# New constants in the table that orders the instructions of all engines: a two-layer attention and GEGLU kernel on one core

## The chip, the cores and the metric

The kernel runs on one core of a Trainium2 chip. A core has five engines with instruction queues of their own: TensorE (PE, with its weight loads shown apart as PEld), VectorE (DVE), ScalarE (ACT), GpSimd (POOL) and SyncE (SP), which only issues DMAs here. Matmuls write into PSUM, eight banks of 128 partitions x 512 fp32; DVE, ACT and POOL work on SBUF, and DVE and ACT read PSUM too. The metric is device microseconds of one execution; three executions of the kernel before gave 2450.06, 2450.28 and 2450.37.

## The reference

A residual block of attention and a residual block of a gated feed-forward network, each behind a layer norm without learned factors, are applied twice with the same weights. There are 2048 rows of 512 numbers, 32 heads of 16, and 1792 hidden columns.

```python
def _A_ref(x, wqkv, wo):                      # H = 32, Dh = 16
    qkv = (x @ wqkv).reshape(B, S, 3, H, Dh).transpose(2, 0, 3, 1, 4)
    q, k, v = qkv[0], qkv[1], qkv[2]
    scores = jnp.einsum("bhqd,bhkd->bhqk", q, k) * (Dh ** -0.5)
    p = _softmax(scores, axis=-1)
    o = jnp.einsum("bhqk,bhkd->bhqd", p, v)
    return o.transpose(0, 2, 1, 3).reshape(B, S, D) @ wo

def _B_ref(x, w_gate, w_up, w_down):
    return (_gelu(x @ w_gate) * (x @ w_up)) @ w_down

x = x + _A_ref(_layernorm(x, axis=-1), A_wqkv, A_wo)
x = x + _B_ref(_layernorm(x, axis=-1), B_w_gate, B_w_up, B_w_down)
x = x + _A_ref(_layernorm(x, axis=-1), A_wqkv, A_wo)
x = x + _B_ref(_layernorm(x, axis=-1), B_w_gate, B_w_up, B_w_down)
```

## The kernel before

The work of attention is cut into units: one block of query rows (512, at the end of the second layer 256, 128 and 128) by four heads, which stand in four groups of 32 partitions. Each unit goes through two passes.

The first pass finds the largest score of each row. PE multiplies 128 query rows with 512 keys for a head (L1910, one PSUM bank), and DVE takes the maximum (L1925), of one bank at a time or of two. To relieve DVE, some of these pieces are folded: POOL forms the difference of two blocks of keys (KD, L1522), PE multiplies it (L1725), ACT keeps its positive part (L1735), and one instruction of DVE (L1920, with a read of its accumulator) then gets the maximum of both blocks from one bank.

The second pass computes the scores again, transposed and with the maximum subtracted (L1782; a bank holds a tile, which is 1, 2 or 4 matmuls of 512, 256 or 128 columns). ACT takes the exponential of one bank or of two (L1758), and PE multiplies it with V and a column of ones (L1806) into the last bank. ACT copies the finished sums out (L1300), POOL divides (L1310, L1315).

Between these, as short chains of matmuls (L769), run the projections to K, Q and V, the output projection, and the feed-forward: the gate matmuls (WG) with GELU on ACT, the up matmuls (WU) with a product (on DVE L1473, or by ACT and POOL L1479 and L1481), the down matmuls (WD) and the addition to x (L1499 in the last layer, which also stores). For most rows GELU is made of tanh (L1394), which stands in the same table of ACT as the exponential. For the last 512 rows of the second layer the GELU table is loaded (L1460): once for 384 rows, in a run of 14 activations during which no exponential is issued, and once for the last 128 rows at the very end. Where PE would idle, it gets fill matmuls on zero weights (L1949), which compute nothing.

All this is put in order before the kernel runs, by a planner in Python. It keeps a clock for each engine with estimated durations, and at each step picks what PE does next: a piece of the first pass, of the second, both, a matmul of a chain, a product with V, or a fill. The instructions of the other engines follow from that. Each engine then runs its list from front to back and waits on semaphores. What the planner picks depends on 33 constants: how many banks each pass may hold (C1, C2 and their like), how long it waits for a second free bank before it takes one (S1D, DB1, S2D, DB2), how far one pass may run ahead of the other (LAG, LAGT, FL, GL), how soon chains are urgent (DUE, DUEM), how many matmuls of a chain go at once (PIECE, GP), and others. A row of the table PLAN holds a set of them. The first pass has 2048 pairs of score blocks; after every 16 of them, a stretch, the planner takes the next row:

```python
if pos["p1"] >= STRETCH * stretch[0]:
    if stretch[0] < len(PLAN):
        SPC, SPLIT, S1C, S2C, OV, LIM, NT, ..., CM, J1, J2 = PLAN[stretch[0]]
    stretch[0] += 1
```

A fill is issued only when PE's load over the last 3.4 us of the planner's clock is below a bound, which isn't in the table.

Of the kernel before, what the change touches and what calls it, by code (L numbers as in the profile page):

```python
# [22 lines left out]
    (0.15, 0.1, 0.55, 0.22, 0.0, -0.05, 2, 0, 30, 84, 13, 80, 0.2, 2.0, -5, 10, 1, 3, 7, 3, 0.1, 4, 3, 3, 3, 4, 0.42, 0.0, 0.42, 0.0, 2, 9.0, 9.0),  # L23
    (0.15, 0.1, 0.55, 0.32, 0.1, 0.0, 3, 0, 30, 50, 13, 80, 0.2, 2.0, 20, 10, 2, 1, 7, 2, 0.0, 4, 3, 3, 4, 4, 0.42, 0.0, 0.42, 0.0, 2, 9.0, 9.0),
    (0.15, 0.1, 0.55, 0.22, 0.0, -0.05, 2, 0, 30, 84, 13, 80, 0.2, 2.0, -5, 10, 2, 3, 7, 3, 0.1, 4, 3, 3, 3, 4, 0.6, 0.0, 0.42, 0.0, 2, 9.0, 9.0),
    (0.15, 0.1, 0.55, 0.22, 0.0, -0.05, 2, 0, 30, 84, 13, 80, 0.2, 2.0, -5, 10, 2, 3, 7, 3, 0.1, 4, 3, 3, 3, 4, 0.6, 0.0, 0.42, 0.0, 2, 9.0, 9.0),
    (0.15, 0.05, 0.55, 0.02, 0.0, -0.05, 3, 0, 30, 76, 13, 80, 0.3, 2.5, -5, 10, 2, 4, 7, 1, 0.1, 4, 3, 3, 3, 4, 0.6, 0.0, 0.42, 0.0, 2, 9.0, 9.0),
    (0.15, 0.05, 0.55, 0.02, 0.0, -0.05, 3, 0, 30, 76, 13, 80, 0.3, 2.5, -5, 10, 2, 4, 7, 1, 0.1, 4, 3, 3, 3, 4, 0.6, 0.0, 0.42, 0.0, 2, 9.0, 9.0),
    (0.15, 0.05, 0.55, 0.32, 0.0, -0.05, 2, 0, 30, 76, 13, 80, 0.2, 3.0, -5, 10, 2, 3, 3, 3, 0.1, 4, 3, 3, 3, 4, 0.8, 0.15, 0.42, 0.0, 2, 9.0, 1.1),
    (0.15, 0.05, 0.55, 0.02, 0.0, -0.1, 3, 0, 30, 76, 13, 80, 0.3, 2.5, -5, 10, 2, 3, 7, 3, 0.1, 4, 3, 2, 3, 4, 0.6, 0.0, 0.42, 0.15, 2, 9.0, 1.1),  # L30
    (0.15, 0.05, 0.55, 0.02, 0.0, -0.05, 3, 0, 30, 76, 13, 80, 0.3, 2.5, -5, 10, 2, 4, 7, 3, 0.1, 4, 3, 3, 3, 4, 0.6, 0.0, 0.42, 0.0, 2, 9.0, 9.0),
    (0.15, 0.05, 0.55, 0.32, 0.0, -0.05, 3, 0, 30, 76, 13, 80, 0.3, 2.5, 10, 10, 2, 3, 7, 3, 0.1, 4, 3, 3, 3, 4, 0.6, 0.0, 0.42, 0.0, 2, 9.0, 9.0),
    (0.15, 0.05, 0.55, 0.32, 0.0, -0.05, 2, 0, 30, 76, 13, 50, 0.2, 3.0, -5, 10, 2, 3, 9, 3, 0.1, 4, 3, 3, 3, 4, 0.8, 0.15, 0.42, 0.0, 2, 1.1, 9.0),
# [3 lines left out]
    (0.15, 0.05, 0.55, 0.32, 0.0, -0.1, 3, 0, 30, 76, 13, 80, 0.3, 2.5, 10, 10, 2, 3, 7, 3, 0.1, 4, 3, 3, 3, 4, 0.6, 0.0, 0.42, 0.0, 2, 9.0, 9.0),  # L37
    (0.15, 0.05, 0.55, 0.32, 0.0, -0.1, 3, 0, 30, 76, 13, 80, 0.3, 2.5, 10, 10, 2, 3, 7, 3, 0.1, 4, 3, 3, 3, 4, 0.6, 0.0, 0.42, 0.0, 2, 9.0, 9.0),
    (0.15, 0.05, 0.55, 0.32, 0.0, -0.05, 2, 0, 30, 76, 13, 80, 0.2, 3.0, -5, 10, 2, 3, 3, 3, 0.1, 4, 3, 3, 3, 4, 0.8, 0.15, 0.42, 0.0, 2, 1.1, 1.1),
    (0.15, 0.05, 0.55, 0.42, 0.2, -0.05, 2, 0, 30, 76, 13, 80, 0.2, 2.0, -5, 6, 2, 3, 3, 3, 0.0, 4, 3, 3, 3, 4, 0.42, 0.0, 0.42, 0.0, 2, 9.0, 9.0),  # L40
    (0.15, 0.05, 0.55, 0.42, 0.1, -0.05, 2, 0, 30, 76, 13, 80, 0.3, 2.0, -5, 6, 2, 2, 5, 3, 0.0, 4, 3, 3, 3, 4, 0.42, 0.0, 0.42, 0.0, 2, 9.0, 9.0),
    (0.15, 0.0, 0.55, 0.42, 0.1, -0.05, 3, 0, 30, 76, 13, 40, 0.7, 2.0, 10, 2, 2, 3, 5, 4, 0.0, 4, 3, 3, 3, 4, 0.42, 0.0, 0.42, 0.0, 2, 9.0, 9.0),
    (0.15, 0.0, 0.55, 0.42, 0.1, -0.05, 3, 0, 30, 76, 13, 40, 0.7, 2.0, 10, 2, 2, 3, 5, 4, 0.0, 4, 3, 3, 3, 4, 0.42, 0.0, 0.42, 0.0, 2, 9.0, 9.0),
    (0.15, 0.05, 0.55, 0.32, 0.0, -0.05, 3, 0, 30, 76, 13, 80, 0.3, 2.5, 10, 10, 2, 3, 7, 3, 0.1, 4, 3, 3, 3, 4, 0.6, 0.0, 0.42, 0.0, 2, 9.0, 9.0),
    (0.15, 0.05, 0.55, 0.32, 0.1, -0.1, 3, 0, 30, 50, 13, 80, 0.3, 2.0, 20, 10, 2, 1, 7, 2, 0.05, 4, 3, 3, 4, 4, 0.42, 0.0, 0.8, 0.0, 2, 9.0, 9.0),
# [3 lines left out]
    (0.2, 0.1, 0.65, 0.32, 0.0, -0.05, 2, 0, 5, 84, 13, 80, 0.3, 2.5, 0, -6, 2, 2, 7, 3, 0.1, 4, 3, 3, 3, 4, 0.42, 0.0, 0.42, 0.0, 2, 9.0, 9.0),  # L49
    (0.2, 0.1, 0.65, 0.32, 0.0, -0.05, 2, 0, 5, 84, 13, 80, 0.3, 2.5, 0, -6, 2, 2, 7, 3, 0.1, 4, 3, 3, 3, 4, 0.42, 0.0, 0.42, 0.0, 2, 9.0, 9.0),  # L50
# [6 lines left out]
    (0.15, 0.1, 0.55, 0.32, 0.0, -0.05, 2, 0, 30, 76, 13, 80, 0.2, 3.0, -10, 10, 2, 3, 3, 3, 0.1, 4, 3, 3, 4, 4, 0.8, 0.0, 0.42, 0.0, 2, 9.0, 9.0),  # L57
    (0.15, 0.1, 0.55, 0.32, 0.0, -0.05, 1, 0, 30, 76, 13, 80, 0.2, 3.0, -10, 10, 2, 3, 3, 3, 0.1, 4, 3, 3, 4, 4, 0.8, 0.0, 0.42, 0.0, 2, 9.0, 9.0),
    (0.15, 0.1, 0.55, 0.32, 0.0, -0.05, 1, 0, 30, 76, 13, 80, 0.2, 3.0, -10, 10, 2, 3, 3, 3, 0.1, 4, 3, 3, 4, 4, 0.8, 0.0, 0.42, 0.0, 2, 9.0, 9.0),
# [2139 lines left out]
```

## Time and profile before

| | |
|---|---|
| median of three executions | 2450.28 us |
| the profiled execution | 2451.07 us |
| its span, first to last instruction | 2449.4 us |
| granted TensorE clock | 1.000 |
| PE busy / DVE busy / ACT busy / POOL busy | 2384.1 / 2360.1 / 2349.9 / 1201.8 us |
| instructions of PE / DVE / ACT / POOL in the profile | 29858 / 3255 / 3240 / 1730 |
| read from and written to HBM | 10.22 and 2.10 MB |

An engine is busy from the start to the end of each instruction, with overlaps counted once. Since an instruction of DVE or ACT can start before the one ahead of it has ended, a row with a mean duration says less than the distance from start to start within a run. A row of a group gives its line, engine, operation and tiles, then its shape and count, then busy time and mean duration, then the idle time just before its instructions and who ended it. A row of the timeline gives the start, the length from the start of the first to the end of the last, and the count of instructions that stand together; its shape is that of the first of them. The last engine instruction ends at 2449.4 us; the first pass ends at 2399.6, where DVE's last maximum stands.

### The profile page before, as it was taken

What the parts mean: (1) busy time and instruction counts of PE and PEld (TensorE: products, weight loads), DVE (VectorE), ACT (ScalarE), POOL (GpSimd) and SP (SyncE); (2) the same over time, 40 slices, a digit from 0 to 9 for tenths busy, and PEclk for the clock granted to TensorE, in tenths of its full rate; (3) what the DMA queues carried; (4) which work ended last, traced back from release to release, by engine and by line L of the source; (5) the groups of instructions that cost most, each with busy time, mean ns of one, the idle gap of its engine ahead of it and who ended that gap; (6) DMA issues with size and microseconds to landing.
All of it is one profiled execution on the core that took longest, in us unless ns stands there. A gap on an engine that the chain in (4) does not pass through costs nothing.

```text
span 2449.4 us, 69119 instructions
## 1 busy us (share of the span) xinstructions
PE 2384.1 (97%) x29858; PEld 1124.5 (46%) x29858; DVE 2360.1 (96%) x3255; ACT 2349.9 (96%) x3240; POOL 1201.8 (49%) x1730
## 2 busy tenths in 40 slices
PE   9999999999999999999999999999999999999999
PEld 3444444444444444444433444444444444444655
DVE  8999999999999999999998999999999999999994
ACT  8999999999999999999999999999999999999985
POOL 6112126775567626675324041567516673377740
PEclk9999999999999999999999999999999999999999
DMA  3020000000100001000100000000001000000000
GB/s 96 33 67 16 5 14 13 5 5 2 22 14 5 5 3 32 4 12 6 26 6 2 9 18 5 14 14 5 7 12 20 5 5 10 17 14 6 13 19 12
DMA packets 72541, 36.65 MB, mean 15 GB/s; under 512 B 54572, under 2 KB 71212, under 8 KB 72236
## 3 DMA queue, kind: packets, MB, share of 16 engines
q1 hardware_dynamic: 72236, 32.23, 5.7%
q8 instruction: 234, 3.83, 0.7%
q14 instruction: 71, 0.58, 0.1%
HBM read 10.22 MB, written 2.10 MB: 5 GB/s over the span
## 4 chain that ended last, share of the span: by engine, by line
PE 49%; DVE 29%; ACT 21%; issue 1%; DMA 0%; POOL 0%; ACTq 0%; DVEq 0%
DVE PM L1925 28%; ACT SCR L1758 18%; PE PS L1910 17%; PE PS L769 12%; PE PS L1806 12%; PE PS L1949 4%; PE PS L1782 4%; ACT SCR L1735 1%; DVE SCR L1920 1%; PE PS L1725 0%; ACT SG L788 0%; ACT ACCS L1300 0%; ACT AO L1479 0%; DMA KT<-SG 0%; PE PS L966 0%
## 5 line engine op out<-in xcount | busy, mean ns | idle before, releaser
L1925 DVE TENSOR_REDUCE PM<-PS 128x1 f32<-128x512 f32 (+1 forms) x2613 | 2158.1, 892 | 41.6 <-PE PS L1782 22.4
L1758 ACT ACTIVATE SCR<-PS 128x1024 bf16<-128x1024 f32 (+1 forms) x2526 | 2024.6, 891 | 55.5 <-PE PS L1782 42.0
L1910 PE MATMUL PS<-KT,QT 32*128 32x512 bf16 x3865 | 1040.4, 384 | 40.0 <-DVE PM L1925 15.6
L1782 PE MATMUL PS<-QT,KT 32*128 32x512 bf16 (+2 forms) x5120 | 941.6, 340 | 2.9 <-ACT SCR L1758 2.1
L1806 PE MATMUL PS<-VP,SCR 128*128 128x51 bf16 (+1 forms) x16384 | 793.0, 187 | 10.0 <-ACT SCR L1758 5.9
L1806 PEld LDWEIGHTS PS<-VP,SCR 128*128 128x128 bf16 x16384 | 564.1, 96 | 480.4 <-issue 401.4
L1910 PEld LDWEIGHTS PS<-KT,QT 32*128 32x128 bf16 x3865 | 249.3, 91 | 550.0 <-DVE PM L1925 255.3
L1949 PE MATMUL PS<-WV,ZER 128*128 128x240 bf16 x2064 | 384.3, 266 | 4.3 <-ACT ACCS L1300 2.1
L1310 POOL TENSOR_TENSOR RL<-ACCS,CM 128x16 f32<-128x16 f32 (+2 forms) x71 | 182.5, 2571 | 328.4 <-ACT ACCS L1300 327.8
L1782 PEld LDWEIGHTS PS<-QT,KT 32*128 32x128 bf16 x5120 | 252.5, 91 | 57.8 <-ACT SCR L1758 27.4
L1949 PEld LDWEIGHTS PS<-WV,ZER 128*128 128x128 bf16 x2064 | 158.8, 96 | 88.4 <-issue 74.2
L1481 POOL TENSOR_TENSOR HT<-HT,AO 128x512 bf16<-128x512 bf16 (+1 forms) x100 | 115.4, 1156 | 87.8 <-ACT AO L1479 87.6
L1920 DVE CUSTOM_DVE_ANT_0 SCR<-PS,SCR 128x512 bf16<-128x512 f32 x231 | 150.1, 686 | 6.0 <-PE PS L1782 3.3
L1199 POOL TENSOR_TENSOR PM<-PM 128x16 f32<-128x16 f32 (+3 forms) x142 | 32.4, 228 | 247.5 <-DVE PM L1925 238.1
L1330 POOL TENSOR_TENSOR X<-X,AO 128x512 f32<-128x512 f32 x47 | 59.5, 1266 | 151.7 <-ACT AO L1328 151.7
L1522 POOL TENSOR_TENSOR KD<-KT 128x512 bf16<-128x512 bf16 x80 | 92.0, 1152 | 82.8 <-PE PS L1725 57.2
L769 PE MATMUL PS<-XNT,WU 128*128 128x512 f16 (+2 forms) x504 | 131.2, 357 | 0.4 <-DVE PM L1925 0.4
L769 PE MATMUL PS<-WD,HT 128*128 128x512 bf16 x448 | 130.2, 381 | 0.2 <-DVE PM L1925 0.2
L769 PE MATMUL PS<-XNT,WG 128*128 128x512 f16 (+2 forms) x504 | 128.0, 357 | 0.3 <-ACT HT L1460 0.2
L1735 ACT ACTIVATE SCR<-PS 128x1024 bf16<-128x1024 f32 (+1 forms) x131 | 125.0, 963 | 2.8 <-PE PS L1725 2.3
L1404 POOL TENSOR_TENSOR HT<-HT,XN 128x512 bf16<-128x512 bf16 x84 | 97.0, 1154 | 6.3
L1391 POOL TENSOR_TENSOR XN<-XN,HT 128x512 f16<-128x512 f16 x84 | 96.9, 1153 | 5.8
(136 smaller groups left out, 1360.4 us busy)
## 6 DMA issues: line engine op xcount, KB each, us to landing
KT<-SG SPq DMA_DIRECT2D x64, 64.0 KB
QT<-SG SPq DMA_DIRECT2D x56, 64.0 KB
out_dram<-AO SPq DMA_DIRECT2D x16, 128.0 KB, 1.7
WG<-in_B_w_gate_dram SPq DMA_DIRECT2D x4, 448.0 KB, 5.0
WU<-in_B_w_up_dram SPq DMA_DIRECT2D x4, 448.0 KB, 4.1
WD<-in_B_w_down_dram SPq DMA_DIRECT2D x4, 384.0 KB, 4.6
MTX<-MSEL SPq DMA_TRANSPOSE x71, 2.2
HT<-in_A_x_dram SPq DMA_DIRECT2D x2, 512.0 KB, 8.6
```

The lines of the kernel that those rows point to most:

```text
L769: ins = e.matmul(out_ap, lhsT=l, rhs=r_, start=(i == 0), stop=(i == n - 1))
L1310: emit("pool", lambda e: e.tensor_tensor(RL[:, s, 0:4 * nq], lsum, AP(CM1, 0, [[1, 128], [0, 4 * nq]]), op=ALU.pow), r=[("ACCS", s), ("CM1 ...
L1404: emit("pool", lambda e, g=g, t=t: e.tensor_tensor(g, g, t, op=ALU.mult), r=gk + tk, w=gk, dur=0.18 + n / 520.0)
L1481: emit("pool", lambda e, ft=ft, o=o: e.tensor_tensor(HT[:, ft, c0:c0 + n], HT[:, ft, c0:c0 + n], AO[:, o, 0:n], op=ALU.mult), r=[("AO", o) ...
L1735: emit("act", lambda e: e.activation(PT[:, s0:s0 + cnt, :], banks(bk), ACTF.Relu), r=bks, w=[("PT", s0 + d) for d in range(cnt)], dur=0.05 ...
L1758: emit("act", lambda e: e.activation(dst, src, ACTF.Exp, scale=DH ** -0.5), r=[BK[b] for b in bk], w=[("PT", i) for i in slots], dur=sw + ...
L1782: ins = e.matmul(bank(bk)[:, i * n:(i + 1) * n], lhsT=KT[32 * j:32 * j + 32, g, kt * 128:(kt + 1) * 128], rhs=QT[32 * j:32 * j + 32, s, 0: ...
L1806: ins = e.matmul(acc, lhsT=PT[:, slot, i * n + qt * 128:i * n + (qt + 1) * 128], rhs=AP(VP, (kt * H + 4 * g + j) * 17, [[NTT * H * 17, 128 ...
L1910: ins = e.matmul(bank(b), lhsT=QT[32 * j:32 * j + 32, s, qt * 128:(qt + 1) * 128], rhs=KT[32 * j:32 * j + 32, g, kb * 512:(kb + 1) * 512], ...
L1920: emit("dve", lambda e, i=i, b=b, sl=sl: e.tensor_tensor_reduce(PT[:, sl, :], bank(b), PT[:, sl, :], 1.0, -3.0e38, ALU.add, ALU.max, po[:, ...
L1925: emit("dve", lambda e: e.tensor_reduce(po, banks(bs), axis=AX.X, op=ALU.max), r=bks, w=[("PM", sm) + h[1:] for h in hs], dur=0.063 + cnt ...
L1949: return e.matmul(PS[:, b, NACC:512], lhsT=ZER[:, :], rhs=WV[:, 0, 0:512 - NACC], start=(b != 7), stop=(b != 7), skip_group_check=True)
```

## The change

Only PLAN changes. It has 129 rows before and after, of which 69 differ: 54 of rows 0 to 80, five of rows 81 to 114, and ten of the last fourteen. Two rows, of stretch 1 and stretch 127:

```diff
-    (0.15, 0.1, 0.55, 0.32, 0.1, 0.0, 3, 0, 30, 50, 13, 80, 0.2, 2.0, 20, 10, 2, 1, 7, 2, 0.0, 4, 3, 3, 4, 4, 0.42, 0.0, 0.42, 0.0, 2, 9.0, 9.0),
+    (0.15, 0.1, 0.55, 0.62, 0.1, 0.0, 3, 0, 30, 50, 13, 80, 0.2, 2.0, 20, 10, 2, 1, 7, 2, 0.0, 4, 3, 3, 4, 4, 0.42, 0.0, 0.42, 0.0, 2, 9.0, 9.0),
...
-    (0.1, 0.05, 0.55, 0.42, 0.7, -0.15, 2, 0, 62, 84, -2, 100, -0.3, 2.5, 20, 6, 2, 2, 11, 1, 0.0, 4, 3, 3, 4, 5, 0.6, 0.0, 0.42, 0.0, 2, 9.0, 9.0),
+    (0.1, 0.35, 0.55, 0.42, 0.7, -0.05, 2, 0, 62, 84, -2, 100, -0.3, 2.5, 20, 6, 2, 1, 11, 1, 0.0, 4, 3, 3, 4, 5, 0.42, 0.0, 0.42, 0.0, 2, 9.0, 9.0),
```

What is computed stays the same, in other sizes and another order. Counted over the whole order:

| instructions | before | after |
|---|---|---|
| DVE L1925, maximum of one bank | 1592 | 1488 |
| DVE L1925, maximum of two banks | 1021 | 1067 |
| DVE L1920, fold | 231 | 237 |
| ACT L1758, exponential of two banks | 1570 | 1563 |
| ACT L1758, exponential of one bank | 956 | 970 |
| ACT L1735, positive part of two banks | 100 | 103 |
| PE L1949, fill | 2064 | 1993 |
| PE, changes between 32-row and full matmuls | 5320 | 5236 |

By sixteenths of the first pass, one-bank maxima become fewer by 40, 27 and 34 in the first, second and tenth, and by 19 in the last; in the others the count changes by 8 at most. In the eleventh to the fourteenth no count of the table differs by more than 3.

The first place is DVE in the first layer's first units, about a sixteenth of the way into the first pass, behind its 212th block of scores. L1925 is the maximum of one bank (128x1) or two (128x2), L1920 a fold and the read of its accumulator. Before:

```order
L1925 TENSOR_REDUCE PM<-PS 128x1 x20
L1920 ISA SCR,PM<-PS,SCR 128x512
L1920 ISA PM 128x1
L1920 ISA SCR,PM<-PS,SCR 128x512
L1920 ISA PM 128x1
L1925 TENSOR_REDUCE PM<-PS 128x1 x12
```

After, at the 234th block:

```order
L1920 ISA PM 128x1
L1925 TENSOR_REDUCE PM<-PS 128x2
L1925 TENSOR_REDUCE PM<-PS 128x1
L1925 TENSOR_REDUCE PM<-PS 128x2
L1925 TENSOR_REDUCE PM<-PS 128x1
L1925 TENSOR_REDUCE PM<-PS 128x2
```

One-bank maxima in runs of 20 and 12 have become an alternation of one two-bank and one one-bank maximum, which goes on for nine two-bank ones.

The second place is the GELU of the 384 rows, shortly before the end. First PE: L769 with WG are its gate matmuls, with WU the up matmuls behind them, L1910 the last pieces of the first pass, L1782 the tiles of the second. Before:

```order
L1949 MATMUL PS<-WV,ZER 128x240 x5
L1910 MATMUL PS<-KT,QT 128x512 x2
L1949 MATMUL PS<-WV,ZER 128x240
L769 MATMUL PS<-XNT,WG 128x384 x2
L1910 MATMUL PS<-KT,QT 128x512 x2
L769 MATMUL PS<-XNT,WG 128x384 x54
L1782 MATMUL PS<-QT,KT 128x128 x16
L769 MATMUL PS<-XNT,WU 128x384 x16
```

After:

```order
L1910 MATMUL PS<-KT,QT 128x512 x2
L769 MATMUL PS<-XNT,WG 128x384 x5
L1910 MATMUL PS<-KT,QT 128x512 x2
L769 MATMUL PS<-XNT,WG 128x384 x9
L1910 MATMUL PS<-KT,QT 128x512 x2
L769 MATMUL PS<-XNT,WG 128x384 x6
L1910 MATMUL PS<-KT,QT 128x512 x2
L769 MATMUL PS<-XNT,WG 128x384 x4
L1910 MATMUL PS<-KT,QT 128x512 x2
L769 MATMUL PS<-XNT,WG 128x384 x5
L1910 MATMUL PS<-KT,QT 128x512 x2
L769 MATMUL PS<-XNT,WG 128x384 x25
```

One pair of first-pass pieces stood behind the first two gate matmuls; now six pairs stand among the first 31 of the 56.

Then ACT at the same place: L1460 is the GELU with its table load, L1758 the exponentials behind it (with the exponential's table load), L1300 the copy of a unit's sums. Before:

```order
L1300 ACTIVATE ACCS<-PS 128x68
L1460 ACT_TABLE_LOAD
L1460 ACTIVATE HT<-PS 128x384 x14
L1758 ACT_TABLE_LOAD
L1758 ACTIVATE SCR<-PS 128x1024 x10
L1300 ACTIVATE ACCS<-PS 128x68
L1758 ACTIVATE SCR<-PS 128x1024 x6
```

After:

```order
L1735 ACTIVATE SCR<-PS 128x512 x4
L1460 ACT_TABLE_LOAD
L1460 ACTIVATE HT<-PS 128x384 x14
L1758 ACT_TABLE_LOAD
L1758 ACTIVATE SCR<-PS 128x1024
L1758 ACTIVATE SCR<-PS 128x512 x2
L1758 ACTIVATE SCR<-PS 128x1024
L1300 ACTIVATE ACCS<-PS 128x68
L1758 ACTIVATE SCR<-PS 128x1024 x6
L1758 ACTIVATE SCR<-PS 128x512 x2
L1758 ACTIVATE SCR<-PS 128x1024
L1300 ACTIVATE ACCS<-PS 128x68
```

Behind the GELU stood 16 two-bank exponentials, which is 32 tiles. Now there are 22 two-bank and 7 one-bank ones (13 and 3 more follow the rows shown), which is 51 tiles.

The third place is the end of PE's list: L1806 are the last products with V, L966 transposes, WO the output projection of the last 128 rows, WG, WU and WD with 128 the feed-forward of these rows, WD otherwise that of the 384 rows, 14 matmuls for each 128 rows. Before:

```order
L769 MATMUL PS<-XNT,WU 128x384 x6
L1949 MATMUL PS<-WV,ZER 128x240
L966 MATMUL PS<-IDN,ATT 128x128 x4
L1949 MATMUL PS<-WV,ZER 128x240 x6
L769 MATMUL PS<-WO,ATTT 128x512 x4
L1949 MATMUL PS<-WV,ZER 128x240 x2
L769 MATMUL PS<-WD,HT 128x512 x18
L966 MATMUL PS<-IDN,XN 128x128 x4
L769 MATMUL PS<-WD,HT 128x512 x4
L769 MATMUL PS<-XNT,WG 128x128 x56
L769 MATMUL PS<-XNT,WU 128x128 x56
L769 MATMUL PS<-WD,HT 128x512 x34
```

After:

```order
L1806 MATMUL PS<-VP,SCR 128x3x17 x12
L1806 MATMUL PS<-VP,SCR 128x51 x4
L769 MATMUL PS<-WD,HT 128x512 x6
L966 MATMUL PS<-IDN,ATT 128x128 x4
L769 MATMUL PS<-WD,HT 128x512 x4
L769 MATMUL PS<-WO,ATTT 128x512 x4
L769 MATMUL PS<-WD,HT 128x512 x18
L966 MATMUL PS<-IDN,XN 128x128 x4
L769 MATMUL PS<-WD,HT 128x512 x4
L769 MATMUL PS<-XNT,WG 128x128 x56
L769 MATMUL PS<-XNT,WU 128x128 x56
L769 MATMUL PS<-WD,HT 128x512 x14
```

Of the 34 down matmuls that stood in the last row, 14 are left there; the other 20 now stand ahead of the last block's gate matmuls.

## What I predict, and how

> **What bounds the kernel now.** I read the page first: the busy time of each engine and its course over the span.
>
> ```profile
> span 2449.4 us, 69119 instructions
> ...
> PE 2384.1 (97%) x29858; PEld 1124.5 (46%) x29858; DVE 2360.1 (96%) x3255; ACT 2349.9 (96%) x3240; POOL 1201.8 (49%) x1730
> ...
> DVE  8999999999999999999998999999999999999994
> ACT  8999999999999999999999999999999999999985
> ...
> PEclk9999999999999999999999999999999999999999
> ...
> PE 49%; DVE 29%; ACT 21%; issue 1%; DMA 0%; POOL 0%; ACTq 0%; DVEq 0%
> ```
>
> Three engines are full at once, from the second slice to the last but one; POOL and the DMA are not near it. The chain that ends last hops between the three (its shares are in the last row). So there is no single bound to relieve: work taken from one engine is worth something only if the other two can follow. Next the busy time by stretches, to see where any of them idles: a steady stretch, the seam between the layers, the end.
>
> ```profile
> 122.00:184.00 62.00, 61.40 (x783) 29.29 (x781) 61.62 (x104) 61.38 (x75) 11.03 (x17) 1.00 0.22 66
> ...
> 1225.00:1286.00 61.00, 59.51 (x538) 23.52 (x536) 56.79 (x92) 55.02 (x85) 14.99 (x39) 1.00 0.03 6
> 1286.00:1347.00 61.00, 60.57 (x641) 23.35 (x640) 53.78 (x75) 55.07 (x84) 26.35 (x30) 1.00 0.01 2
> ...
> 2388.00:2450.00 62.00, 57.90 (x690) 35.12 (x686) 27.26 (x58) 36.18 (x63) 5.39 (x12) 1.00 0.04 12
> ```
>
> After the length come PE, its weight loads, DVE and ACT. In the steady row DVE and ACT idle for 0.4 and 0.6 us of 62. At the seam they idle for 4.2 and 6.0, then 7.2 and 5.9 us of 61; in the last row for 34.7 and 25.8 of 62. Something can be won without less work only at the seam and at the end.
>
> **The change: the exchange of sizes.** Counted over the whole order, DVE's maxima (L1925) go from 1592 one-bank and 1021 two-bank ones to 1488 and 1067, and the folded pieces (L1920 on DVE, L1735 on ACT) from 231 to 237. ACT's exponentials (L1758) go from 1570 two-bank and 956 one-bank ones to 1563 and 970, its folds from 100 two-bank ones to 103. PE's matmuls of real work stay the same; the fills (L1949) go from 2064 to 1993. The groups by shape price these:
>
> ```profile
> L1925 DVE TENSOR_REDUCE PM<-PS 128x2 f32<-128x1024 f32 x1021 | 1243.0, 1219 | 30.8 <-PE PS L1782 17.9 <-PE PS L1910 4.5
> L1925 DVE TENSOR_REDUCE PM<-PS 128x1 f32<-128x512 f32 x1592 | 1045.5, 682 | 10.8 <-PE PS L1782 4.5 <-PE PS L1910 2.4 <-PE PS L1725 0.8
> L1920 DVE CUSTOM_DVE_ANT_0 SCR<-PS,SCR 128x512 bf16<-128x512 f32 x231 | 150.1, 686 | 6.0 <-PE PS L1782 3.3 <-PE PS L1910 1.6
> L1920 DVE DVE_READ_ACCUMULATOR2_ANT PM<- 128x1 f32 x231 | 19.3, 83 | 0.0
> ```
>
> ```profile
> L1758 ACT ACTIVATE SCR<-PS 128x1024 bf16<-128x1024 f32 x1570 | 1548.4, 1056 | 45.5 <-PE PS L1782 35.0 <-PE PS L1910 0.2
> L1758 ACT ACTIVATE SCR<-PS 128x512 bf16<-128x512 f32 x956 | 562.5, 620 | 10.0 <-PE PS L1782 7.0 <-PE PS L1910 0.3
> L1735 ACT ACTIVATE SCR<-PS 128x1024 bf16<-128x1024 f32 x100 | 106.8, 1070 | 1.4 <-PE PS L1725 0.9 <-PE PS L1910 0.4
> ```
>
> By these mean durations DVE gets -104 x 0.682 + 46 x 1.219 + 6 x (0.686 + 0.083) = -10.2 us, and ACT -7 x 1.056 + 14 x 0.620 + 3 x 1.070 = +4.5 us. But the durations overlap, as runs of one shape in the timeline show:
>
> ```profile
> 1383.66 7.87 DVE L1925 TENSOR_REDUCE PM<-PS 128x1 f32<-128x512 f32 x13 [0.18 <-PE PS L1910]
> ...
> 2394.03 2.92 DVE L1925 TENSOR_REDUCE PM<-PS 128x2 f32<-128x1024 f32 x3
> ```
>
> ```profile
> 66.60 16.66 ACT L1758 ACTIVATE SCR<-PS 128x1024 bf16<-128x1024 f32 x18 [2.01 <-PE PS L1782]
> ```
>
> ```profile
> 302.00 0.69 DVE L1920 CUSTOM_DVE_ANT_0 SCR<-PS,SCR 128x512 bf16<-128x512 f32 x1
> ...
> 302.61 0.69 DVE L1920 CUSTOM_DVE_ANT_0 SCR<-PS,SCR 128x512 bf16<-128x512 f32 x1
> ```
>
> ```profile
> 1208.76 6.63 ACT L1758 ACTIVATE SCR<-PS 128x512 bf16<-128x512 f32 x13
> ```
>
> From start to start a one-bank maximum takes (7.87 - 0.68) / 12 = 0.60 us; the three of the second row are two two-bank ones and a one-bank one, so a two-bank one takes (2.92 - 0.68) / 2 = 1.12; a two-bank exponential (16.66 - 1.06) / 17 = 0.92, a one-bank one (6.63 - 0.62) / 12 = 0.50; a fold 302.61 - 302.00 = 0.61. By these steps DVE gets -62.4 + 51.5 + 3.7 = -7.2 us and ACT -6.4 + 7.0 + 2.8 = +3.4. So DVE loses between 7.2 and 10.2 us of work and ACT gains between 3.4 and 4.5: taken in the middle, -8.7 and +3.9. Some evictions change engine (two up-projection tiles from ACT and POOL to DVE, two others from DVE to ACT); they cancel within 0.3 us. The two engines end together and the order is free to shift waiting between them, so I count the mean: (-8.7 + 3.9) / 2 = **-2.4 us**, between -1.9 and -2.9 if both ends go together. SP issues the same 525 instructions, and POOL three memsets more and two products less.
>
> [...]
>
> **PE's stretches.** PE changes between the 32-row matmuls and full ones 5320 times before and 5236 times after, so 42 visits to the 32-row mode go, and 71 fills.
>
> ```profile
> PEld PS L1806 <- issue: 401.4, 1681, 0.4
> ...
> ACT SCR L1758 <- PE PS L1782: 42.0, 144, 2.0
> ...
> DVE PM L1925 <- PE PS L1782: 22.4, 89, 1.8
> ```
>
> The first row prices a visit: 401.4 / 1681 = 0.24 us in which no weights can be loaded for the products with V, so PE gets 42 x 0.24 = 10.0 us. DVE and ACT wait for PE's scores for 22.4 and 42.0 us in all, so what comes through lies between 0 and 10.0 x 0.49 = 4.9 us (PE's share of the chain). Most of the merged maxima stand where DVE and ACT hardly wait, as in the steady row; I take **-1.0 us**. The seam is ordered anew too, but nothing in the order says how its 11 to 12 us of idle time change: 0, between -6 (half of it) and +4.
>
> **The end.** The last 56 us are one sequence: the GELU of 384 rows, the last exponentials, the last block.
>
> ```profile
> 2393.34 1.28 ACT L1460 ACT_TABLE_LOAD   x1
> 2398.12 0.49 ACT L1460 ACTIVATE HT<-PS 128x384 bf16<-128x384 f32 x1 [3.50 <-PE PS L769]
> ...
> 2408.37 9.47 ACT L1758 ACTIVATE SCR<-PS 128x1024 bf16<-128x1024 f32 x10
> ...
> 2417.85 5.85 ACT L1758 ACTIVATE SCR<-PS 128x1024 bf16<-128x1024 f32 x6
> ```
>
> ```profile
> 2399.67 0.18 DVE L1230 TENSOR_REDUCE MSEL<-PM 128x4 bf16<-128x16 f32 x1
> ...
> 2408.11 2.09 DVE L1473 TENSOR_TENSOR HT<-PS,HT 128x384 bf16<-128x384 f32 x4 [7.25 <-PE PS L769]
> ```
>
> ```profile
> 2422.28 0.34 PE PS L1782 x8
> 2422.62 0.31 PE PS L1806 x8
> 2422.94 1.30 PE PS L769 x8
> ...
> 2427.79 3.88 PE PS L769 x18
> 2431.68 0.22 PE PS L966 x4
> 2431.90 14.47 PE PS L769 x150
> ...
> 2446.45 0.69 DVE AO L1499
> ```
>
> Behind the GELU stand 32 score tiles now (10 + 6 two-bank exponentials) and 51 in the changed order. Two tiles cost PE 0.34 + 0.31 and two up-projection matmuls, 0.33 (8 take 1.30): 0.98 us, and ACT the same, since its run of 10 takes 0.95 each. So 19 more tiles lengthen this part by 9.5 x 0.98 = 9.3 us, and ahead of the GELU ACT is rid of 9.5 x 0.92 = 8.7 us. What is queued behind them waits with them: the last unit's normalization, its output projection and the last block. In turn 20 of the 34 down-projection matmuls leave the last run of PE; at 3.88 / 18 = 0.216 us that is -4.3 us, if DVE's last products (L1473) aren't late for the 14 that remain; they follow the up-projection matmul by matmul, and the down-projection can begin with the first of them. So from the table load to the end it is 56.1 + 9.3 - 4.3 = 61.1 us, and the question is how much earlier the load comes. By ACT 8.7 us: net -3.7. By DVE, five two-bank maxima more stand between the gate matmuls, where DVE now waits for 7.25 us: the load can come 5 x 1.12 = 5.6 us earlier for the same DVE, net -0.6. I take **-2.0 us**, between the two; if the load came no earlier, it were +5.0.
>
> The sum is -2.4 - 1.0 - 2.0 = -5.4 us. The profiled execution took 2451.07 us (span 2449.4 and 1.7 around it) and goes to 2445.7; the median of the runs is 0.8 lower, 2450.28, and goes to **2444.9**.
>
> **The rivals.** (1) ACT holds the time: it gets 3.9 us more work and is as full as DVE; with the end by its own reckoning, -3.7, the sum is +0.2: 2450.5. For it speaks that ACT's row is level with DVE's; against it, that ACT waits for scores twice as long (42.0 against 22.4 us), which better placed work can use up. (2) PE was the hidden bound: its share of the chain, 49%, comes through whole: -2.4 - 4.9 - 3.7 = -11.0: 2439.3. Against it: PE has 2064 fills to drop. (3) Slower: the load of the GELU table comes no earlier, because the gate matmuls need the last rows' projection and that hangs on PE and POOL; the 19 tiles then lengthen the end by +5.0, with nothing won before it 2455.3. It decides from the point where the load comes less than 5.0 us earlier than now. Against it speak the 7.25 us in which DVE idles there.
>
> (4) The clock: it is granted in full in every slice, and 38 of the 71 fills that go stand in the last sixteenth of the score work. If PE fell to half the clock in its last run, the 10.2 us that remain of it were doubled: 2445 + 10 = 2455. [...] (5) The change doesn't show, because the eleventh to the fourteenth sixteenth keep nearly their order (no count differs by more than 3) and what is won before them is waited away there: 2450.3.
>
> **How the numbers follow.** About 0.2%, 4.9 us, is what a measurement of this kernel can tell from no change. The forecast gets 0.50, with 2442 to 2448.5 as its own range; seven tenths of it lie beyond 4.9 us. Rival 1 gets 0.20, rival 2 0.16, rival 3 0.09, rival 4 0.03, rival 5 0.02. Faster: 0.35 + 0.16 = 0.51; the same: 0.15 + 0.20 + 0.02 = 0.37; slower: 0.12. The range leaves out rivals 3 and 4 and the far half of rival 2 with the seam's gain on top: 2437 to 2451.5.
>
> **What would show it.** DVE busy near 2350 to 2353 us and ACT near 2353 to 2355; the table load of the last GELU 7 us earlier before the end's 61; PE's last run near 10 us instead of 14.47, and DVE idle for less than 4 us during the GELU. If DVE's idle time grows by what its work fell, rival 1 holds; if the visits' 0.24 us show as shorter waits of ACT for PE, rival 2. I am wrong altogether if the seam moves by more than 6 us, for which I have no row.

## The result, and the profile after

The changed kernel took **2432.72 us** (median of 12 runs) where the kernel before took 2450.43 (12 runs): a ratio of 0.9932, 95% interval 0.9921 to 0.9943, or 17.7 us less. The prediction had 2444.9 and a range of 2437 to 2451.5. The direction was right, the size less than a third of it, and the time lies outside the range. The profiled execution took 2432.66 us, with a span of 2430.9. The ratio compares means, without one execution of before that took 2603.99 us and with one of the changed kernel at 2446.29; by medians it is 0.9928.

The page of the changed kernel: span, busy time of the engines, and the shares of the chain that ended last.

```profile
span 2430.9 us, 68920 instructions
...
PE 2366.8 (97%) x29787; PEld 1120.1 (46%) x29787; DVE 2350.8 (97%) x3209; ACT 2348.0 (97%) x3250; POOL 1202.3 (49%) x1731
...
PE 44%; DVE 31%; ACT 24%; issue 1%; DMA 0%; POOL 0%; SPq 0%; ACTq 0%; DVEq 0%
```

DVE's busy time fell by 9.3 us, as the counts had it; ACT's fell by 1.9, though it got more work. PE's fell by 17.3, of which the 71 fills explain some 7 (one starts 0.10 us after the other); its first-pass matmuls (L1910), 6 fewer of 3865, are busy for 17.2 us less, since they stand more densely, so PE's busy time is no measure of its work either. The groups by shape (count, busy us, mean ns, then the idle time just before):

```profile
L1925 DVE TENSOR_REDUCE PM<-PS 128x2 f32<-128x1024 f32 x1067 | 1297.9, 1217 | 26.6 <-PE PS L1782 14.6 <-PE PS L1910 3.1
L1925 DVE TENSOR_REDUCE PM<-PS 128x1 f32<-128x512 f32 x1488 | 981.9, 680 | 8.0 <-PE PS L1782 3.8 <-PE PS L1910 0.9 <-PE PS L1725 0.2
```

```profile
L1758 ACT ACTIVATE SCR<-PS 128x1024 bf16<-128x1024 f32 x1563 | 1542.9, 1063 | 34.7 <-PE PS L1782 26.4
L1758 ACT ACTIVATE SCR<-PS 128x512 bf16<-128x512 f32 x970 | 571.2, 624 | 8.9 <-PE PS L1782 5.3 <-PE PS L1910 0.3
```

Single instructions last as long as before, to 7 ns; the idle time ahead of them is what shrank, from 30.8 to 26.6 and 10.8 to 8.0 us on DVE, from 45.5 to 34.7 and 10.0 to 8.9 on ACT. The waits say the same (us in total, times, longest):

```profile
PEld PS L1806 <- issue: 395.5, 1666, 0.4
PEld PS L1910 <- DVE PM L1925: 263.1, 806, 0.9
ACT SCR L1758 <- PE PS L1782: 31.7, 119, 0.7
DVE PM L1925 <- PE PS L1782: 18.5, 73, 1.7
```

ACT waits for score tiles 10.3 us less than before, DVE 3.9. The second row closes the ring: PE's weight loads for the first pass wait for DVE to free a bank.

The seam, in two stretches of 61 us (length, then PE, weight loads, DVE, ACT, POOL busy), and the end as ACT, DVE and the chain show it:

```profile
1215.00:1276.00 61.00, 60.61 (x550) 24.50 (x547) 57.20 (x93) 56.86 (x95) 24.69 (x54) 1.00 0.05 11
1276.00:1337.00 61.00, 60.20 (x657) 25.39 (x653) 55.33 (x74) 55.18 (x85) 24.89 (x31) 1.00 0.01 2
```

```profile
2369.04 1.28 ACT L1460 ACT_TABLE_LOAD   x1
2372.02 0.49 ACT L1460 ACTIVATE HT<-PS 128x384 bf16<-128x384 f32 x1 [1.70 <-PE PS L769]
```

```profile
2383.73 2.51 DVE L1473 TENSOR_TENSOR HT<-PS,HT 128x384 bf16<-128x384 f32 x4 [3.23 <-PE PS L769]
...
2427.74 0.69 DVE L1499 TENSOR_TENSOR AO<-PS,X 128x512 bf16<-128x512 f32 x1 [2.73 <-PE PS L769]
```

```profile
2417.57 10.15 PE PS L769 x130
2427.72 0.02 issue
```

At the seam DVE idles for 3.8 and 5.7 us, ACT for 4.1 and 5.8, two us less in all than before on each. From the table load to the end of the span it is 2430.9 - 2369.0 = 61.9 us, and the load comes 24.3 us earlier.

**Where the time went.** The idle time of a row leaves out a part of the waiting. Packed one-bank maxima start every 0.597 us and last 0.68, packed one-bank exponentials start every 0.477 us and last 0.62: if the next one is late by less than 0.08 us (DVE) or 0.14 us (ACT), it still starts before the one ahead has ended, and the engine never counts as idle. So I took from the trace, for each instruction of DVE and ACT, the distance to the next start, called its work the distance within which the shortest tenth of its shape stays (1.131 us for a two-bank maximum, 0.904 for a two-bank exponential), and the rest a wait. Work and waits of an engine then add up to the span. Before, DVE waited 138 us of 2449 and ACT 192, where the page shows 89 and 100 us idle. The difference, after minus before, by sixteenths of the first pass (256 of its 4096 blocks each, by DVE's progress; us):

| sixteenths | length before | length | DVE work | DVE waits | ACT work | ACT waits |
|---|---|---|---|---|---|---|
| 1 to 4 | 581.7 | -2.5 | -0.5 | -2.0 | -0.8 | -1.8 |
| 5 to 10 | 913.8 | -10.5 | -4.5 | -6.0 | +2.6 | -13.1 |
| 11 to 14 | 582.9 | -0.4 | -0.5 | 0.0 | +0.4 | -0.9 |
| 15, 16 and the end | 371.0 | -4.9 | -1.7 | -3.2 | +1.0 | -5.9 |
| all | 2449.4 | -18.4 | -7.1 | -11.3 | +3.3 | -21.7 |

The work changed as predicted by the steps (-7.2 and +3.4). What the prediction didn't have is the two columns of waits. Within the second row, the ninth sixteenth, which holds the seam, gives only -1.0; the tenth gives -3.3 and the eighth -2.5.

### The profile page after: what moved, and what is told of

Read it like the earlier page. It is cut to its first block, busy times and chain, and to the rows that moved or that the text cites. A ratio compares the mean times of both kernels' runs of the same rounds, so it can differ in the third digit from the quotient of the medians.

```text
span 2430.9 us, 68920 instructions
## 1 busy us (share of the span) xinstructions
PE 2366.8 (97%) x29787; PEld 1120.1 (46%) x29787; DVE 2350.8 (97%) x3209; ACT 2348.0 (97%) x3250; POOL 1202.3 (49%) x1731
## 4 chain that ended last, share of the span: by engine, by line
PE 44%; DVE 31%; ACT 24%; issue 1%; DMA 0%; POOL 0%; SPq 0%; ACTq 0%; DVEq 0%
DVE PM L1925 30%; ACT SCR L1758 21%; PE PS L1910 15%; PE PS L769 11%; PE PS L1806 10%; PE PS L1782 4%; PE PS L1949 4%; ACT SCR L1735 2%; DVE SCR L1920 1%; PE PS L1725 1%; ACT AO L1479 0%; ACT SG L788 0%; ACT XN L1394 0%; ACT AO L1328 0%; ACT ACCS L1300 0%
## 5 line engine op out<-in xcount | busy, mean ns | idle before, releaser
L1925 DVE TENSOR_REDUCE PM<-PS 128x1 f32<-128x512 f32 (+1 forms) x2555 | 2144.0, 905 | 34.6 <-PE PS L1782 18.5
L1758 ACT ACTIVATE SCR<-PS 128x1024 bf16<-128x1024 f32 (+1 forms) x2533 | 2024.4, 895 | 43.5 <-PE PS L1782 31.7
L1910 PE MATMUL PS<-KT,QT 32*128 32x512 bf16 x3859 | 1023.2, 384 | 41.1 <-DVE PM L1925 17.9
L1782 PE MATMUL PS<-QT,KT 32*128 32x512 bf16 (+2 forms) x5120 | 939.7, 340 | 2.0 <-ACT SCR L1758 1.0
L1806 PE MATMUL PS<-VP,SCR 128*128 128x51 bf16 (+1 forms) x16384 | 790.0, 187 | 8.5 <-ACT SCR L1758 4.8
L1806 PEld LDWEIGHTS PS<-VP,SCR 128*128 128x128 bf16 x16384 | 564.8, 96 | 471.5 <-issue 395.5
L1910 PEld LDWEIGHTS PS<-KT,QT 32*128 32x128 bf16 x3859 | 245.5, 91 | 547.4 <-DVE PM L1925 263.1
L1949 PE MATMUL PS<-WV,ZER 128*128 128x240 bf16 x1993 | 374.3, 266 | 3.7 <-ACT SCR L1758 2.3
L1782 PEld LDWEIGHTS PS<-QT,KT 32*128 32x128 bf16 x5120 | 252.0, 91 | 58.5 <-ACT SCR L1758 24.4
L1949 PEld LDWEIGHTS PS<-WV,ZER 128*128 128x128 bf16 x1993 | 153.1, 96 | 81.1 <-issue 67.1
L1920 DVE CUSTOM_DVE_ANT_0 SCR<-PS,SCR 128x512 bf16<-128x512 f32 x237 | 153.2, 686 | 4.9 <-PE PS L1782 1.6
L1481 POOL TENSOR_TENSOR HT<-HT,AO 128x512 bf16<-128x512 bf16 x98 | 113.7, 1163 | 78.3 <-ACT AO L1479 77.9
L1199 POOL TENSOR_TENSOR PM<-PM 128x16 f32<-128x16 f32 (+3 forms) x142 | 32.6, 230 | 232.7 <-DVE PM L1925 224.7
L1735 ACT ACTIVATE SCR<-PS 128x1024 bf16<-128x1024 f32 (+1 forms) x134 | 129.9, 981 | 3.1 <-PE PS L1725 2.5
L769 PE MATMUL PS<-XNT,WU 128*128 128x512 f16 (+2 forms) x504 | 130.9, 357 | 0.6 <-DVE PM L1925 0.4
L769 PE MATMUL PS<-WD,HT 128*128 128x512 bf16 x448 | 129.0, 381 | 0.4 <-DVE PM L1925 0.4
L769 PE MATMUL PS<-XNT,WG 128*128 128x512 f16 (+2 forms) x504 | 128.2, 357 | 0.2 <-DVE PM L1925 0.2
```

The costliest lines, as they stand in the source:

```text
L769: ins = e.matmul(out_ap, lhsT=l, rhs=r_, start=(i == 0), stop=(i == n - 1))
L1481: emit("pool", lambda e, ft=ft, o=o: e.tensor_tensor(HT[:, ft, c0:c0 + n], HT[:, ft, c0:c0 + n], AO[:, o, 0:n], op=ALU.mult), r=[("AO", o) ...
L1735: emit("act", lambda e: e.activation(PT[:, s0:s0 + cnt, :], banks(bk), ACTF.Relu), r=bks, w=[("PT", s0 + d) for d in range(cnt)], dur=0.05 ...
L1758: emit("act", lambda e: e.activation(dst, src, ACTF.Exp, scale=DH ** -0.5), r=[BK[b] for b in bk], w=[("PT", i) for i in slots], dur=sw + ...
L1782: ins = e.matmul(bank(bk)[:, i * n:(i + 1) * n], lhsT=KT[32 * j:32 * j + 32, g, kt * 128:(kt + 1) * 128], rhs=QT[32 * j:32 * j + 32, s, 0: ...
L1806: ins = e.matmul(acc, lhsT=PT[:, slot, i * n + qt * 128:i * n + (qt + 1) * 128], rhs=AP(VP, (kt * H + 4 * g + j) * 17, [[NTT * H * 17, 128 ...
```

## The experiments

Three theories at first. W: the new order leaves shorter waits in the stretches whose rows changed. P: PE was the bound, and fewer fills and fewer visits to the 32-row mode came through. D: DVE's work counts in full. Each run is compared with the kernel before on the same chip:

| run | median us | before us | ratio (95%) |
|---|---|---|---|
| rows 0 to 80 new | 2438.61 | 2450.84 | 0.9950 (0.9934 to 0.9967) |
| rows 81 to 128 new | 2445.10 | 2450.84 | 0.9977 (0.9967 to 0.9986) |
| every tenth fill out | 2448.05 | 2450.84 | 0.9988 (0.9979 to 0.9998) |
| 201 memsets on DVE | 2450.92 | 2450.84 | 1.0000 (0.9991 to 1.0009) |
| 101 activations on ACT | 2453.69 | 2450.18 | 1.0014 (1.0006 to 1.0023) |
| 100 maxima more on DVE | 2456.69 | 2450.18 | 1.0025 (1.0015 to 1.0035) |
| rows 48 to 80 new | 2488.13 | 2450.18 | 1.0156 (1.0143 to 1.0170) |
| new table, every tenth fill out | 2432.78 | 2450.18 | 0.9928 (0.9915 to 0.9942) |
| old table shifted | 2482.89 | 2450.27 | 1.0134 (1.0117 to 1.0151) |
| new table shifted | 2489.00 | 2450.27 | 1.0162 (1.0146 to 1.0177) |
| every third pair of banks split | 2458.03 | 2450.27 | 1.0033 (1.0020 to 1.0046) |
| new table, no fills | 2686.69 | 2450.27 | 1.0963 (1.0935 to 1.0991) |
| rows 0 to 27 new | 2450.03 | 2450.34 | 0.9999 (0.9990 to 1.0008) |
| rows 0 to 26 new | 2499.59 | 2450.34 | 1.0202 (1.0188 to 1.0216) |
| rows 34 to 80 new | 2440.54 | 2450.34 | 0.9962 (0.9950 to 0.9975) |

### Which half of the table

```diff
-PLAN = [old rows 0 to 128]
+PLAN = [new rows 0 to 80, old rows 81 to 128]
```

> The kernel before with rows 0 to 80 of the changed table (up to about 1500 us of the span) and its own rows behind them. Its order has 40 fewer visits of PE to the 32-row mode and 30 fewer fills than before. Theory W (the new order of the early stretches leaves shorter waits there, and they are the gain): the first pass passes its ten sixteenths some 14 us earlier, as in the changed kernel, and the whole takes 2436 to 2438 us. Rival E (nearly all of the 17.7 us comes from the end, where the last rows changed): 2447 to 2450.

```diff
-PLAN = [old rows 0 to 128]
+PLAN = [old rows 0 to 80, new rows 81 to 128]
```

> The kernel before with rows 81 to 128 of the changed table alone. Theory W: only the end gains, some 4 to 5 us: 2445 to 2446.5. Rival E: 2433 to 2436. If the two parts help each other, this one and the run with rows 0 to 80 together give less than 17.7 us.

They gave -12.2 and -5.7 us, together -17.9 where the whole change gave -17.7; the first is 0.6 us above theory W's range, the second within it. In the first run the sixteenths 11 to 16 keep their lengths of before to 0.2 us; in the second all ahead of the thirteenth keep theirs to 0.5. So the gain is local, and more than two thirds of it lie ahead of the end. In the second run the table load of the GELU stands at

```profile
2381.84 1.28 ACT L1460 ACT_TABLE_LOAD   x1
```

which is 11.5 us earlier than before (2393.34) by the new end alone, and its span ends 61.6 us later.

### What an engine's work costs

First PE, with every tenth fill left out; then DVE with 201 one-column memsets.

```diff
 def warm_emit(b):
-    emit_pe(warm_fn(b), 1, 512 - NACC, r=[("ZER",), ("WV",)], w=[BK[b]])
+    n = n_fill[0]
+    n_fill[0] += 1
+    emit_pe(warm_fn(b), 1, 512 - NACC, r=[("ZER",), ("WV",)], w=[BK[b]], skip=n % 10 == 9)
```

> The kernel before with every tenth fill matmul left out of PE's list (206 of 2064), all else in the same order; the fills compute nothing. That takes 206 x 0.104 = 21 us of work from PE. Theory P (PE was the hidden bound, so its 17 us less busy time are the gain): 2429 to 2435. Theory W (PE only waits elsewhere): 2449 to 2451. By PE's share of the chain, one half: about 2440. If the clock falls for lack of fills, slower, and the granted clock shows it.

```diff
+n_dum[0] += 1
+if n_dum[0] % 13 == 0:
+    sch.op("dve", lambda e: e.memset(KBIAS[:, 1:2], 0.0), w=[("DUM",)])
```

> The kernel before with 201 memsets of one column put behind every thirteenth maximum on DVE, all else in the same order: they compute nothing that is used. Each should cost DVE some 0.06 to 0.1 us, 12 to 20 us in all. Theory D (DVE is the bound, its work counts in full): 2462 to 2470. The mean rule of the prediction: half of that, 2456 to 2460. Theory W (what sets the time is how the order makes the engines wait for each other): below a third, 2450 to 2455.

PE lost some 21 us of work (its busy time fell from 2384.1 to 2362.1, but some 100 matmul records are missing from this trace) and the time fell by 2.8, or 0.13 us for each us (0.02 to 0.25 by the interval). That is against P, and 1 us more than W had. It prices PE's time where the planner put fills, that is, where PE had least to do; no run takes work from PE elsewhere. The memsets say nothing of D: each lasts 59 ns and starts, at the median, 24 ns after the start of the maximum it follows, so that they run beside it and add hardly any work:

```profile
L1931 DVE MEMSET KBIAS<- 128x1 f32 x201 | 11.9, 59 | 0.0
```

So three probes with real work, on ACT, on DVE, and on DVE with its own kind of work:

```diff
+n_dum[0] += 1
+if n_dum[0] % 25 == 0:
+    sch.op("act", lambda e: e.activation(KBIAS[:, 1:2], CM05[:, 0:1], ACTF.Copy), r=[("CM05",)], w=[("DUM",)])
```

> The order of before, and on ACT, behind every 25th exponential, one activation of a 128x1 constant into an unused column: 101 of them, nothing waits for them, and what is computed is unchanged. Small activations of the profile (68 columns) start 0.10 us before the next one and last 0.22, so this is 10 to 20 us of work for ACT. If ACT sets the time through the first pass, +10 to +20 us. If DVE and ACT share the end, as the prediction's mean has it, +5 to +10. If ACT has waits to give (theory: waits for scores, not work, set the pace), +0 to +5.

```diff
+n_dum[0] += 1
+if n_dum[0] % 26 == 0:
+    sch.op("dve", lambda e: e.tensor_reduce(KBIAS[:, 1:2], ZER[:, 0:128], axis=AX.X, op=ALU.max), r=[("ZER",)], w=[("DUM",)])
```

> The order of before, and on DVE, behind every 26th maximum, one maximum over 128 zeros in SBUF: 100 of them, into an unused column, for which nothing waits; what is computed is unchanged. A maximum over 64 numbers lasts 0.18 us and the next instruction starts 0.22 after it, so this is about 20 to 25 us of work, real work this time, unlike the memsets. If DVE sets the time, +18 to +25 us; if the mean of DVE and ACT counts, +9 to +13; if waits set the pace and DVE has them to give, under +6.

```diff
+n_dum[0] += cnt == 2
+two = cnt == 2 and n_dum[0] % 3 == 0
...
+    if two:
+        e.tensor_reduce(po[:, 0:1], bank(bs[0]), axis=AX.X, op=ALU.max)
+        return e.tensor_reduce(po[:, 1:2], bank(bs[1]), axis=AX.X, op=ALU.max)
     return e.tensor_reduce(po, banks(bs), axis=AX.X, op=ALU.max)
```

> The order of before, with every third two-bank maximum done as two one-bank ones (340 of 1021): DVE gets 340 x (2 x 0.597 - 1.131) = +21 us by the steps from start to start, the banks come free together as before, and no other instruction moves. If DVE's work counts in full, +21 us; if half (the prediction's mean), +11; if as the dummy maxima had it (6.5 us for 19), +6 to +8.

The groups of the first two, in the trace of each:

```profile
L1763 ACT ACTIVATE KBIAS<-CM 128x1 f32<-128x1 f32 x101 | 23.3, 230 | 0.0
```

```profile
L1931 DVE TENSOR_REDUCE KBIAS<-ZER 128x1 f32<-128x128 bf16 x100 | 27.5, 275 | 0.0
```

From start to start an activation cost 0.092 us and a maximum 0.192, so ACT got 9.3 us of work and DVE 19.4; the split gave DVE 21.6. The time rose by 3.5, 6.5 and 7.8 us: 0.38, 0.34 and 0.36 us for each us of work, with 0.16 to 0.60, 0.19 to 0.44 and 0.23 to 0.52 from the intervals of the ratios. What doesn't come through is taken out of the engine's own waits: DVE's fell by 14.7 us with the dummy maxima and by 15.2 with the split. D falls. The mean rule of the prediction has 0.5, which lies above all three; the dummy maxima exclude it, the other two intervals alone don't. (6.5 us for the dummy maxima is just above the "under 6" of the theory of waits, too.) At 0.35 for DVE and 0.38 for ACT the exchange of sizes, -7.1 and +3.3 us, is worth -1.2 us by these prices.

### PE in the new order

```diff
-PLAN = [old rows 0 to 128]
+PLAN = [new rows 0 to 128]
...
+    emit_pe(warm_fn(b), 1, 512 - NACC, r=[("ZER",), ("WV",)], w=[BK[b]], skip=n % 10 == 9)
```

> The changed kernel with every tenth fill left out, 198 fewer, 20 us of PE: nothing else moves. If PE's time is no bound, as the same edit on before had it (-2.8 us of 21), -1 to -4 us against the changed kernel, so 2429 to 2432, 18 to 22 us below before. If the new order made PE the bound: -8 us or more. If the granted clock falls below 1.0: slower than the changed kernel.

2432.78 us: PE lost some 20 us of work (busy 2366.8 to 2348.3, with 99 matmul records missing from this trace) and the median stayed that of the changed kernel, 2432.72, where 1 to 4 us less was expected. The ratios, 0.9928 and 0.9932, overlap. But the five executions differ in the granted clock: two at 1.000 took 2431.15 and 2431.35, three at 0.999 took 2432.78 to 2433.72. Set against the changed kernel's 2432.7, the fills are worth some 1.4 us at the full clock, 0.07 for each us, and nothing in the three with the lower one.

### Is it the rows, or where they stand?

```diff
-PLAN = [old rows 0 to 128]
+PLAN = [old rows 0 to 47, new rows 48 to 80, old rows 81 to 128]
```

> Rows 48 to 80 of the new table alone, the others of before: the seventh to the tenth sixteenth, with the seam. Against before: one-bank maxima -10, two-bank -12, folds +17 (DVE's work -9 us, ACT's about +8), fills +93. By the prediction's rule (mean of the two engines, seam at nothing) -1 us. If the gain is local to the stretches whose rows changed, as the lengths of the run with rows 0 to 80 have it (these four sixteenths 8 us shorter), -6 to -10 us. If the gain needs what the rows ahead of it set up, -3 to +3.

No theory had what came: **+38 us**, with rows of which, in their own surroundings, none had lengthened its sixteenth. Over half of it, 20.0 us, stands in the fifteenth sixteenth, whose rows are the old ones. That gave the theory that holds now, F: a row is good only in the state of the queues (banks held, how far one pass is ahead, how far the chains have come) in which it was chosen. To test it, both tables were taken a quarter of a stretch later:

```diff
-if pos["p1"] >= STRETCH * stretch[0]:
+if pos["p1"] >= STRETCH * stretch[0] + 4 * (stretch[0] > 0):
```

> The table of before, each row but the first taken 4 pairs of score blocks later (a quarter of a stretch): the same recipes in nearly the same places, but each begins in another state of the queues than the one in which it stood. One-bank maxima 1602, two-bank 1046, fills 2132. If a row is a good recipe for its region, within 5 us of before. If a row is good only in the state in which it was chosen, as the run with rows 48 to 80 alone (+38 us) has it, +10 to +60 us.

> The new table shifted in the same way. One-bank maxima 1634, two-bank 1036, fills 2140. If the new rows are better recipes (more merges, for example), this stays 10 to 20 us below the shifted old table. If the gain is only that the rows fit the state that each stretch meets, it is gone: as far above before as the shifted old table, within some 15 us either way.

The old table lost 32.6 us and the new one 56.3, from 2432.7 to 2489.0. Shifted, the new one is 6 us slower than the old one: nothing of its advantage is left. Every row is still there; only its moment has moved. That speaks for F, but each table was shifted only once and each row's place moved with its state, so the two shifts alone can't tell place from state, nor rule out that a part of the gain lies in the recipes. In the shifted old table DVE's work rose by 18.2 us and ACT's fell by 12.3; at the prices above that is +1.7 us of 32.6, and the waits make the rest.

Then a single row. In the order of PE, the new rows 0 to 27 followed by the old ones come back to the order of before, word for word; rows 0 to 26 never do.

```diff
-    (0.2, 0.1, 0.65, 0.32, 0.0, -0.05, 2, 0, 5, 84, 13, 80, 0.3, 2.5, 0, -6, 2, 2, 7, 3, 0.1, 4, 3, 3, 3, 4, 0.42, 0.0, 0.42, 0.0, 2, 9.0, 9.0),
+    (0.15, 0.05, 0.55, 0.32, 0.0, -0.1, 3, 0, 30, 76, 13, 80, 0.3, 2.5, 10, 10, 1, 3, 7, 3, 0.1, 4, 3, 3, 3, 4, 0.6, 0.0, 0.42, 0.0, 2, 9.0, 9.0),
```

> Rows 0 to 27 of the new table, before's from there. In the order of PE the last 11396 of its 14481 pieces are those of before word for word, so the new rows end in the state that before's row 28 was chosen for. One-bank maxima 1542, two-bank 1048, fills 2044. If rows fit states: the gain of these stretches alone, the first four sixteenths of the changed kernel, -2.6 us, and the rest unchanged to 0.2 us in each sixteenth: 2447 to 2448.5.

> One row fewer, 0 to 26. Now PE's order doesn't come back to that of before at any place. DVE's sizes differ little from the run with rows 0 to 27 (10 one-bank maxima more, 2 two-bank fewer), fills are 80 more. If the size of the gain lies in the sizes and rows as such: within 3 us of the run with rows 0 to 27. If rows fit states: 2470 to 2495, and the loss lies in sixteenths whose rows are those of before.

```diff
-PLAN = [old rows 0 to 128]
+PLAN = [old rows 0 to 33, new rows 34 to 80, old rows 81 to 128]
```

> Rows 34 to 80 of the new table, before's on both sides; PE's order is before's up to row 34 and its last 5243 pieces are before's. One-bank maxima 1552, two-bank 1036, fills 2054. If the gain is local: that of the fifth to the tenth sixteenth of the changed kernel, -10.5 us, 2439 to 2441. By the prediction's terms (DVE's work -4, ACT's about +2, seam nothing) -1 to -2. If the rows needed what rows 0 to 27 left behind: slower, as the rows 48 to 80 alone.

With row 27 the time is that of before, without it **49 us** longer, 4.6 more than the range that was expected. The rows from 27 on stand there in the places that they have in the kernel before; only the state in which they begin is another. Lengths against before, in us:

| sixteenths | whole change | rows 0 to 27 | rows 0 to 26 | rows 34 to 80 | rows 48 to 80 |
|---|---|---|---|---|---|
| 1 to 4 | -2.5 | -2.7 | -2.1 | -1.4 | -1.3 |
| 5 to 10 | -10.5 | +1.9 | +18.6 | -10.5 | +10.6 |
| 11 to 14 | -0.4 | 0.0 | +11.8 | 0.0 | +6.6 |
| 15, 16, end | -4.9 | 0.0 | +19.4 | 0.0 | +20.7 |

Rows 34 to 80 keep their -10.5 us without anything new ahead of them, since they begin in the old state and end in it. (The -1.4 and -1.3 in rows 1 to 4 of the last two columns stand in the first sixteenth, where their order is that of before; the start of the program varies by that much: the run with the memsets lost 1.6 us there.) Rows 0 to 27 have the gain of their own stretches, -2.7, but the time is -0.3 instead of the -2 to -3 expected: 0.5 us in the sixth and 1.4 in the ninth sixteenth were lost where the order is that of before. Of the 1.4, the trace puts 1.02 to one wait, which ends at 1193.28 us: PE waits for a load of K (KT<-SG). Fifteen of the load's sixteen parts landed 2.2 us earlier than before, like all around them; one landed a microsecond after those, while a 16 KB packet of the instruction queue (q8) took 0.93 us, from 1191.13. In the kernel before no such packet ran beside this load. That the packet held the part up is inferred, not tested. The rest is open.

What a misfit looks like: with rows 0 to 26, in the fifteenth sixteenth, DVE and ACT in turn

```profile
2223.88 2.41 DVE L1925 TENSOR_REDUCE PM<-PS 128x2 f32<-128x1024 f32 x3
...
2231.03 0.69 DVE L786 CAST HT<-PS 128x512 bf16<-128x512 f32 x1 [2.51 <-PE PS L769]
2234.22 0.69 DVE L786 CAST HT<-PS 128x512 bf16<-128x512 f32 x1 [2.51 <-PE PS L769]
2237.42 0.69 DVE L1473 TENSOR_TENSOR HT<-PS,HT 128x512 bf16<-128x512 f32 x1 [2.50 <-PE PS L769]
...
2249.43 3.64 DVE L1925 TENSOR_REDUCE PM<-PS 128x2 f32<-128x1024 f32 x4 [2.27 <-PE PS L1910]
```

```profile
2272.68 0.28 ACT L788 ACTIVATE SG<-PS 128x128 bf16<-128x128 f32 x1
2278.56 4.69 ACT L1758 ACTIVATE SCR<-PS 128x1024 bf16<-128x1024 f32 x5 [5.60 <-PE PS L1782]
```

From 2226.3 to 2249.4 DVE gets no maximum at all: PE issues the second pass and the chains of the feed-forward, and the first pass stands still. Afterwards ACT waits 5.6 us for a tile of the second pass. The run with rows 48 to 80 alone has the same stretch without a maximum, 23.1 us long, from 2214.9 to 2238.0. So the 19.0 and 20.0 us that these two runs lose in the fifteenth sixteenth go with one event that both meet; the shifted tables don't meet it, and their losses are spread over many sixteenths. What in the planner sets it off was not tried. The trace of before has no gap of a microsecond on DVE anywhere from 2180 to 2245 us; its maxima run on:

```profile
2224.65 26.30 DVE L1925 TENSOR_REDUCE PM<-PS 128x1 f32<-128x512 f32 x31
```

The waits of ACT for score tiles show the same over the whole run, 72.8 us where the kernel before has 42.0 and the changed one 31.7:

```profile
ACT SCR L1758 <- PE PS L1782: 72.8, 205, 6.4
```

### Without fills

```diff
-PLAN = [old rows 0 to 128]
+PLAN = [new rows 0 to 128]
...
+    emit_pe(warm_fn(b), 1, 512 - NACC, r=[("ZER",), ("WV",)], w=[BK[b]], skip=True)
```

> The changed kernel without its fills (8 of 1993 stay, at the start): 528 us of PE's time as the profile counts it. If PE's own work bounds and the fills stand in its way, -20 us or more. If fills stand where PE would wait anyway and the clock stays at 1.0, -10 to 0. If the fills hold the clock up (the one run of the changed kernel at 0.925 took 13.6 us longer), a granted clock below 0.97 and +10 us or more.

254 us slower than the changed kernel. The granted clock (tenths, one digit for each slice) shows why:

```profile
PEclk9755556978659677798989765669687797998789
```

Its mean is 0.763. So fills aren't idle ballast: a tenth of them can go at next to no loss of clock (1.000 in all executions of the old order, 0.999 in three of five of the new one), all of them can't.

## Why the prediction was too small

**"Something can be won without less work only at the seam and at the end."** This is the step that failed: it put the waits of the stretches between at nothing, and no term of the sum stands for them. Rows 0 to 80 alone, which leave the end as it was, gave -12.2 us, and rows 34 to 80 alone -9.8, with -1.0 in the sixteenth of the seam. The sentence was read from idle time in windows, 0.4 and 0.6 us of 62 in a steady stretch. By starts, the second sixteenth holds 4.1 us of waits on DVE and 4.7 on ACT in 138, and all sixteenths but the last together some 94 and 155; in the changed kernel they fell. The same holds for ACT's busy time, predicted to rise to 2353 to 2355: it fell to 2348.0 while its work rose by 3.3, because busy time contains waits shorter than the overlap.

**The exchange of sizes: work right, rule wrong.** DVE's busy time is 2350.8 (predicted 2350 to 2353), the work by steps -7.1 and +3.3. A second step failed behind it: "The two engines end together and the order is free to shift waiting between them, so I count the mean." That takes the waits of DVE and ACT together as given. They aren't: they fell by 11.3 and 21.7 us. The price of work came out lower as well, 0.34 to 0.38 for each us instead of 0.5, so this term is about -1.2, not -2.4.

**PE's stretches (-1.0) and rival 2.** The sign that I had named for rival 2, shorter waits of ACT for PE, did appear (42.0 to 31.7 us), but not its cause. Some 21 us less of PE were worth 2.8 us in the old order and some 20 us 0 to 1.4 in the new one, so PE's 17.3 us are worth 0 to -2.2 by the medians, and -4.3 by the far end of the first interval. The price of a visit was misread: the row has 1681 waits beside 2660 visits, so it is not one wait for each, and it fell by 5.9 us, from 401.4 to 395.5, where 10.0 were forecast. Nor does the time follow the visits: the sixth sixteenth lost 20 changes of mode and 0.6 us, the eighth lost 3 and 2.5 us, and the third and fourth gained 11 changes and lost 1.2 us. No run changed the visits alone. So the shorter waits of ACT and DVE come, for the greater part, from better placed scores and not from a relieved PE; this is inferred from what is left.

**The seam (0).** The sign "I am wrong altogether if the seam moves by more than 6 us" missed the point: the ninth sixteenth moved by 1.0, and the unpriced gain lies on both sides of it, -6.2 us in the fifth to the eighth and -3.3 in the tenth. The seam holds a GELU table load as well, at 1263.8 us before and 1250.7 after, with 14 activations of 512 columns and no exponential for some 20 us, which the account of the kernel above leaves out; so the seam had a row to reckon from.

**The end (-2.0).** The mechanism was right: 61.9 us from the table load to the end for 61.1 predicted, PE's last run 10.15 us for about 10, DVE idle 3.23 us for less than 4. The size was off: the last two sixteenths and the end became 4.9 us shorter, since the load moved by some 10 us (11.5 less what was won ahead of it), more than by ACT's reckoning (8.7), which I had averaged with DVE's 5.6. The net by ACT alone, -3.7, was the nearer.

**The other rivals.** ACT didn't hold the time (1): its waits took the extra work and fell besides. The load did come earlier (3). The clock stayed at 1.0 in the profiled run (4). That half of it would double PE's last run (+10 us) was my estimate, which no run shows; half the clock stands in the records of the run without fills, which took 254 us more at a mean of 0.763. What was won early wasn't waited away (5): the eleventh to the fourteenth sixteenth keep their lengths to 0.4 us in all.

Put together, of 18.4 us in the profile about 1.2 are the price of changed work and 0 to 4.3 PE's; the rest, some 13 to 17, is shorter waits, by the order of the end and of the rows ahead of it. Where they lie is shown by the runs with parts of the table; that the worth of a row hangs on the state in which it begins is shown by row 27, and the shifts agree. Which single constant of a row shortens which wait was not tried.

## What to carry to other kernels

Where three engines pass eight banks round a ring, don't price work by its length: here a microsecond on DVE or ACT cost some 0.35 and one of PE's fills 0.13 or less, and a probe that adds a known piece of work tells that price, within an interval (here about 0.2 to 0.5). Look for what a new order can win in the distances from start to start, not in idle time, since waits shorter than the overlap of two instructions (here 0.08 us for one-bank maxima on DVE, 0.14 us for one-bank exponentials on ACT) are counted as busy. And before pricing an edit of a generated order, compare the orders: where the edited piece comes back to the old order word for word, its effect stays local but for a microsecond or two; where it doesn't, stretches that nobody touched can lose more (49 us here, by one row) than the piece can win.

## What the runs showed of the hardware

- A DVE memset of one column runs beside the maximum that it follows: 201 of them, 59 ns each, cost nothing that can be told from noise (2450.92 against 2450.84 us), while maxima over 128 elements of SBUF cost 0.192 us each from start to start, of 0.275 us length.
- Without fills PE was still 96% busy by the profile (2584.7 us of 2683.0) and yet the clock fell to between 0.5 and 0.9 in most slices, so busy time at that scale doesn't tell what holds the clock. In this trace's clock records, finer than the slices, the clock stands at 1.0 or at 0.5 and nothing between, and each of the 91 stretches ahead of the last, which ends with the records, is a whole multiple of 3.41 us. Ahead of each of the 45 falls among them PE was 65 to 94% busy over 3.41 us (median 83%); over the stretches of that length after which the full clock stayed it was 99% busy at the median.
- One of the 12 runs of the changed kernel had a mean clock of 0.925 and took 2446.29 us, 13.6 more than the median, with the same fills. What set it off isn't known.
- The same order repeats closely: where two kernels share the order of a sixteenth, its length mostly agreed to 0.1 us, which makes such tables readable at a tenth of the interval of the whole.
